# One agenda for every step beside the products, and the first chunk's output through x's buffer: sparse attention followed by a gated network

## The chip, the cores and the metric

The kernel runs on one core of a Trainium2 chip. The metric is the device time of one execution in microseconds. Before the change the median of three runs is 885.96 (885.71 to 888.02).

The core's engines work in parallel, each through its own queue in program order: TensorE (PE) multiplies, VectorE (DVE) and ScalarE (ACT) work element by element, GpSimd (POOL) does too, and SyncE (SP) issues transfers. ACT issues transfers as well, from its own queue. An instruction that waits holds everything behind it on its engine.

## What is computed

```python
# attention: q, k, v of (8 batches, 8 heads, 576, 64), stride 32, scale 1/8
rel = pos[:, None] - pos[None, :]
mask_local   = (rel >= 0) & (rel < 32)                       # heads 0 to 3
mask_strided = (rel >= 0) & (pos[None, :] % 32 == pos[:, None] % 32)   # heads 4 to 7
scores = where(mask, scale * q @ k.T, -1e9)
scores -= max(scores);  attn = exp(scores)
attn /= sum(attn) + 1e-9
x = (attn @ v) laid out as (4608 tokens, 512)

# network: w_in (512, 2048), w_out (2048, 512)
h = x @ w_in
g = where(h >= 1, h, where(h <= -1, 0, (h + 1)**2 / 4))
out = g @ w_out
```

## The kernel before

The network's operands are split into a rounded part and a remainder, and each product is three matmuls (`HI_LO`): high by high, high by low, low by high.

**The network.** The 4608 tokens go in two ways. The first three chunks of 512 tokens (`c` = 0, 1, 2) are done plainly: for each of 16 steps `f`, `up(c, f)` makes one 128-row tile of h in 12 matmuls, `gate` bends it (two activations on ACT, one operation on DVE), `rounded` splits it into `gh` (ACT, in chunks 1 and 2) and `gl` (DVE), and `down` adds it to four output tiles in 12 matmuls. `down` runs two steps behind `up`: `pend` holds the tiles between. h has two PSUM banks, so `up` of a step waits until `gl` of two steps earlier has been read from its bank. `gh` and `gl` have three buffers each, taken by `f % 3`.

The other tokens go in three super-chunks of 1024 (`s` = 0, 1, 2) with a seven-product scheme for 2 by 2 blocks: `up_block` has 56 units of six matmuls, `down_block` 28 units of twelve. Its operands are sums of blocks of x (`x_sum` on DVE, and `x_split`, one cast on ACT and one subtraction on DVE) and sums of blocks of the weights. `prep` makes the operands of `down_block` two units ahead. The weights come back from DRAM through a ring of seven buffers on SP (`fetch_w`).

**Work beside the network in chunks 1 and 2.** The rounded weights of each step are stored to DRAM (`ship`, on ACT's queue). For each of 16 pairs of steps and sides, `combine` makes sums of weight blocks on POOL (two operations of 128x512 and four of 128x256), `round_sums` casts them on ACT, `rest_of_sums` subtracts on DVE, and `ship_sums` stores them from ACT's queue. The room for it is one half of an x buffer (`X0` or `X1`), which held the x of chunk 0 or 1 and later holds that of a super-chunk.

**Attention** for batches 1 to 7 is laid beside the network. A batch has four units: 0 and 1 local, 2 and 3 strided. A step is a letter and a unit: s scores (PE), m mask (DVE, out of PSUM), x maximum (DVE), a or b subtract it (POOL or DVE), e exponential (ACT), q sum (DVE), p or k add eps (ACT or DVE), r or w normalise (a reciprocal on DVE, then POOL or DVE), t transpose (DVE), j store the transposed tile to DRAM and J read it back as pT (both SP), v times the values (PE; V does units 1 and 3), h and l copy the result to x as high and low part (ACT, DVE; l does nothing for tokens of the super-chunks). Scores and values share two PSUM banks, "a": each s, v or V takes both, and the next waits until m, or h and l, have read them.

**What sets the order.** The order on every engine is the order in which the program issues instructions. Time is counted in a unit of six matmuls: step `f` of chunk `c` begins at 4 * (16 * (c - 1) + f), chunk 1 at 0, chunk 2 at 64, the first super-chunk at 128, the second at 240. `LATER` is one table of places for all batches 2 to 7, and `START` says where each batch begins; batches 2, 3 and 4 use b and w in place of a and r. `COMBINE`, `X_FIRST` and `X_NEXT` place the sums and x steps. Within a step of chunks 1 and 2 the order is: `up`; scores and values of the step's first half; `gate`; the first half's other attention steps; `ship`; sums; x steps; `rounded`; the whole `down`; then the second half's steps, sums and x steps. Transfers of q, k and v are issued right behind the step that frees their buffer (`after`).

The output of chunk 0 is copied into three small buffers of the pool `o_p` (which the transposed tiles use too), that of chunk 1 into half 0 of `X1`, that of chunk 2 into a buffer of its own; `put` stores each of the four tiles from SP.

Of the kernel before, what the change touches and what calls it, by code (L numbers as in the profile page):

```python
# [25 lines left out]
def tile_sparse_attention_then_ffn(
# [274 lines left out]

    def fetch_v(b, *parts):
        for u, k in parts:
            if 0 < b < B and (b, UNITS[u][0], UNITS[u][1] + k * VB) not in loaded:
                load_v(b, u, k)


    def attention(b, kinds):
# [256 lines left out]
        def low(u):  # L565
            if u not in flipped:
                return
            for src, to in parts(u):
# [4 lines left out]
        steps = {"s": score, "y": score_0, "z": score_1, "m": mask, "o": opened, "i": cover, "g": plain, "x": most, "w": norm_v, "a": below_max, "e": expo, "q": total, "p": plus_eps, "k": plus_eps_v, "b": below_max_v, "r": norm,
                 "f": flip, "t": turn, "j": spread, "J": gather, "c": keep, "d": keep_v, "v": value, "V": values_1_3, "h": high, "l": low}
        after = {"s1": lambda: fetch_qk(b, 2), "s3": lambda: b > 1 and fetch_qk(b + 1, 0),
                 "v0": lambda: fetch_v(b, (1, 0), (2, 0))}
        if b == 1:
            after |= {"v1": lambda: fetch_v(b, (3, 0)), "v2": lambda: fetch_v(b + 1, (0, 0)), "v3": lambda: fetch_v(b + 1, (0, 1))}
        else:
            after |= {"v2": lambda: fetch_v(b, (3, 0)), "V1": lambda: fetch_v(b + 1, (0, 0), (0, 1))}  # L580
# [59 lines left out]
    def put(rows, cols, t):  # L640
        nc.sync.dma_start(out[rows * P:(rows + 1) * P, cols:cols + CH], t)

    def down(c, f, gs):
        if f == 0:
            o_ps[c] = [psum("o", [P, CH], f"o_{c}_{d}") for d in range(NC)]
        if f == NF - 1 and c:
            room = x_tile(1)[:, 0] if c == 1 else slot(HL_AT[0], [P, NC, CH], F32, f"ob_{c}")
        for d in range(NC):
            h, e = divmod(d * P, HF)
            for n, (x, y) in enumerate(HI_LO):  # L650
                nc.tensor.matmul(o_ps[c][d], wt[f][:, 1, h, x, e:e + P], gs[y],  # L651
                                 start=f == 0 and n == 0, stop=f == NF - 1 and n == 2)
# [231 lines left out]
    with tc.manual_schedule():  # L884
# [38 lines left out]
        goes = {b: attention(b, lambda u, kind, n: "a") for b in range(1, B)}  # L923

        def steps(g0, g1, which):
            for b, g in START.items():
                for at, names in LATER.items():
                    if g0 <= g + at < g1:
                        goes[b](names[which] if b > 4 else names[which].replace("a", "b").replace("r", "w"))

        def x_steps(s, *todo):
            for m in todo:
                x_split(m, s) if m > 0 else x_sum(-m, s)

        COMBINE = {h: (n // NP, n % NP, half) for n, (h, half) in enumerate((
            (0, 1), (2, 0), (5, 1), (7, 0), (10, 1), (12, 0), (15, 1), (20, 1),
            (32, 1), (35, 0), (37, 1), (40, 0), (42, 1), (47, 1), (52, 1), (57, 1)))}

        def sums(h):
            for at, do in ((h - 5, ship_sums), (h - 4, rest_of_sums), (h - 3, round_sums), (h, combine)):
                if at in COMBINE:
                    i, j, half_ = COMBINE[at]
                    do(i, j, x_tile(at // 32)[:, half_])

        X_FIRST = {50: (1,), 52: (2,), 61: (-7, -6, 7), 62: (-4, -5, 6), 63: (5,)}
        pend = []
        for c in range(CLASSIC):
            for f in range(NF):  # L950
# [3 lines left out]
                pe, pre, mid, post = ("",) * 4 if c else STEPS.get(f, ("",) * 4)
                go = goes[1]
                go(pe)
                if c:
                    steps(g0, g0 + 2, 0)
                else:
# [16 lines left out]
                go(post)
                if c:
                    steps(g0, g0 + 2, 1)
                    ship(f, c - 1)
                    sums(g0 // 2)  # L980
                    x_steps(0, *X_FIRST.get(g0 // 2, ()))
                if c:
                    pend.append((c, f, rounded(c, f)))
                if len(pend) > 2:
                    down(*pend.pop(0))
                if c or f == NF - 1:
                    steps(g0 + 2, g0 + 4, 0)
                    steps(g0 + 2, g0 + 4, 1)
                    sums(g0 // 2 + 1)
                    x_steps(0, *X_FIRST.get(g0 // 2 + 1, ()))  # L990
        for n in range(3):
            fetch_w(n)
        for n, a in enumerate(pend):
            down(*a)
# [4 lines left out]
        for s in range(NSC):
            g0 = 4 * NF * (CLASSIC - 1) + 2 * len(UP) * s  # L1000

            def beside(n):
                for which in range(2):
                    steps(g0 + n, g0 + n + 1, which)

            up_block(s, beside)

            def beside_down(n):
                for which in range(2):
                    steps(g0 + len(UP) + 2 * n, g0 + len(UP) + 2 * n + 2, which)  # L1010
                if s + 1 < NSC:
                    x_steps(s + 1, *X_NEXT.get(n, ()))

            down_block(s, beside_down)
# [58 lines left out]
```

## Time and profile before

| what | us |
|---|---|
| median of three runs | 885.96 |
| the profiled execution | 881.21 |
| its span, first to last instruction | 879.1 |
| chunk 1's first step up begins at | 118.89 |
| chunks 1 and 2 take, to the first super-chunk | 251.4 |
| first super-chunk takes | 180.9 |
| second | 169.2 |
| third, to the end of the span | 158.7 |

The stages are read from the begin of each stage's first matmul. The mean granted TensorE clock of the execution is 0.984 of full. The profile's busy time of an engine doesn't tell how fast it worked: a matmul under a low clock is busy longer. A wait is shown with the one that ended it last ("releaser"). A name with an arrow, out<-in, gives the tile written and those read: `h` is a step up, `o` a step down, `sc` scores, `xp` values, `xs` an x buffer in its later use, `hl` the operands of a super-chunk's way down.

### The profile page before, as it was taken

What the parts mean: (1) busy time and instruction counts of PE and PEld (TensorE: products, weight loads), DVE (VectorE), ACT (ScalarE), POOL (GpSimd) and SP (SyncE); (2) the same over time, 40 slices, a digit from 0 to 9 for tenths busy, and PEclk for the clock granted to TensorE, in tenths of its full rate; (3) what the DMA queues carried; (4) which work ended last, traced back from release to release, by engine and by line L of the source; (5) the groups of instructions that cost most, each with busy time, mean ns of one, the idle gap of its engine ahead of it and who ended that gap; (6) DMA issues with size and microseconds to landing.
All of it is one profiled execution on the core that took longest, in us unless ns stands there. A gap on an engine that the chain in (4) does not pass through costs nothing.

```text
span 879.1 us, 17888 instructions
## 1 busy us (share of the span) xinstructions
PE 825.4 (94%) x6965; PEld 662.0 (75%) x6965; DVE 575.3 (65%) x846; ACT 498.6 (57%) x876; POOL 216.0 (25%) x220
## 2 busy tenths in 40 slices
PE   8999998858998899999999989999999899999997
PEld 6688886746876777777877857788888578888885
DVE  6899857655546555855767677566577854467564
ACT  6889835342435534666866533567854437676442
POOL 6364451762025524312321000131110001111000
PEclk9999999978999899999999999999999999999999
DMA  9917226765647865897997846788656567666664
GB/s 354 408 64 271 86 97 236 264 242 190 199 156 257 276 217 213 294 281 242 295 297 232 254 145 225 251 249 241 209 187 215 157 226 210 191 194 190 216 207 141
DMA packets 101795, 195.10 MB, mean 222 GB/s; under 512 B 17104, under 2 KB 32464, under 8 KB 99664
## 3 DMA queue, kind: packets, MB, share of 16 engines
q1 hardware_dynamic: 92496, 164.60, 58.1%
q10 hardware_dynamic: 9216, 29.36, 8.8%
q8 instruction: 55, 0.90, 0.4%
q14 instruction: 28, 0.23, 0.1%
HBM read 147.26 MB, written 46.66 MB: 221 GB/s over the span
## 4 chain that ended last, share of the span: by engine, by line
PE 61%; DVE 18%; ACT 10%; DMA 5%; issue 3%; POOL 1%; SPq 1%; ACTq 0%; DVEq 0%; POOLq 0%
PE y L748 13%; PE h L606 10%; PE o L651 10%; PE yo L849 8%; PE z L748 7%; DVE hl L702 5%; PE xo L849 4%; ACT hl L701 3%; PE x L748 3%; PE xp L507 3%; PE sc L344 2%; DMA pT<-there 2%; DMA ks<-xs 2%; DVE xs L254 1%; DVE xs L698 1%
## 5 line engine op out<-in xcount | busy, mean ns | idle before, releaser
L606 PE MATMUL h<-xq,w 128*128 128x512 f32 x576 | 146.5, 404 | 9.6 <-DVE gl L637 8.8
L748 PE MATMUL y<-x,wr 128*128 128x512 f32 x576 | 140.7, 391 | 0.4 <-ACT ga L756 0.4
L849 PE MATMUL yo<-hl,wr 128*128 128x512 f32 x576 | 135.0, 392 | 3.6 <-DVE hl L702 3.6
L606 PEld LDWEIGHTS h<-xq,w 128*128 128x128 f32 x576 | 109.9, 194 | 36.8 <-DVE gl L637 11.0
L651 PE MATMUL o<-gh,w 128*128 128x512 f32 x384 | 131.9, 405 | 0.5 <-ACT ob L655 0.5
L849 PEld LDWEIGHTS yo<-hl,wr 128*128 128x128 f32 x576 | 107.3, 188 | 29.2 <-DVE hl L702 6.5
L748 PEld LDWEIGHTS y<-x,wr 128*128 128x128 f32 x576 | 107.6, 188 | 23.6 <-ACT ga L756 0.9
L651 PEld LDWEIGHTS o<-gh,w 128*128 128x128 f32 x384 | 74.0, 193 | 18.0 <-ACT ob L655 1.4
L849 PE MATMUL zo<-hl,wr 128*128 128x512 f32 x288 | 69.8, 395 | 8.5 <-DVE hl L702 4.6
L651 PE MATMUL o<-gl,w 128*128 128x512 f32 x192 | 76.4, 398 | 0.4 <-DVE gl L637 0.4
L748 PE MATMUL z<-x,wr 128*128 128x512 f32 x288 | 74.3, 393 | 1.7 <-ACT gab L783 1.3
L245 POOL TENSOR_TENSOR xs<-w 128x512 f32<-128x512 f32 x32 | 44.8, 1421 | 113.5 <-DMA ks<-xs 66.1
L849 PEld LDWEIGHTS zo<-hl,wr 128*128 128x128 f32 x288 | 53.3, 188 | 24.4 <-DVE hl L702 7.5
L702 DVE TENSOR_TENSOR hl<-ga,hl 128x1024 fp32r<-128x1024 f32 x36 | 45.0, 1249 | 40.2 <-ACT hl L701 40.2
L616 DVE SCALAR_TENSOR_TENSOR h<-h,u 128x512 f32<-128x512 f32 x47 | 32.8, 697 | 54.8 <-ACT u L613 54.5
L701 ACT CAST hl<-ga 128x1024 fp32r<-128x1024 f32 x36 | 38.0, 1055 | 53.2 <-DVE ga L802 29.4
L748 PEld LDWEIGHTS z<-x,wr 128*128 128x128 f32 x288 | 53.4, 188 | 13.8 <-ACT gab L783 1.8
L613 ACT ACTIVATE tmp<-tmp 128x512 f32<-128x512 f32 x96 | 60.7, 632 | 3.1
L788 POOL TENSOR_TENSOR ga<-gb,ga 128x1024 f32<-128x1024 f32 x9 | 21.6, 2405 | 165.5 <-DVE ga L616 157.7
L410 POOL TENSOR_TENSOR pr<-pr,st 128x768 f32<-128x768 f32 (+3 forms) x19 | 23.6, 1242 | 136.3 <-DVE st L406 135.4
L247 POOL TENSOR_TENSOR xs<-xs 128x256 f32<-128x256 f32 x64 | 54.6, 853 | 5.0
L610 ACT ACTIVATE u<-h,half 128x512 f32<-128x512 f32 x48 | 32.8, 684 | 36.5 <-PE h L606 27.4
(117 smaller groups left out, 1310.3 us busy)
## 6 DMA issues: line engine op xcount, KB each, us to landing
wr<-ks SPq DMA_DIRECT2D x192, 256.0 KB, 3.7
wr<-kq SPq DMA_DIRECT2D x144, 256.0 KB, 3.0
ks<-xs ACTq DMA_DIRECT2D x16, 1024.0 KB, 4.1
raw<-in_w SPq DMA_DIRECT2D x30, 512.0 KB, 9.6
kq<-w ACTq DMA_DIRECT2D x48, 256.0 KB, 3.2
qk<-in_qk_s SPq DMA_DIRECT2D x16, 604.0 KB, 6.3
qk<-in_qk_l SPq DMA_DIRECT2D x16, 576.0 KB, 6.0
v<-in_v_l SPq DMA_DIRECT2D x21, 384.0 KB, 5.1
```

The costliest lines, as they stand in the source:

```text
L245: nc.gpsimd.tensor_tensor(out=b[:, :, f] if i else b[:, f], in0=hi, in1=lo, op=ALU.add)
L247: nc.gpsimd.tensor_tensor(out=st[:, to, HF:], in0=st[:, x, HF:], in1=st[:, y, HF:], op=op)
L507: nc.tensor.matmul(xp[p][j * D:(j + 1) * D, n], loaded[b, local, b0 + n][keys, j], qs, start=True, stop=True)
L606: nc.tensor.matmul(o_ps[c, f], wt[f][:, 0, h, x, e:e + P], xq[c][:, y, cc], start=first and n == 0, stop=last and n == len(todo) - 1)
L610: nc.scalar.activation(u, h, AF.Relu, bias=half, scale=0.5)
L613: nc.scalar.activation(u, u, AF.Square)
L616: nc.vector.scalar_tensor_tensor(out=to, in0=h, scalar=1.0, in1=u, op0=ALU.max, op1=ALU.min)
L651: nc.tensor.matmul(o_ps[c][d], wt[f][:, 1, h, x, e:e + P], gs[y], start=f == 0 and n == 0, stop=f == NF - 1 and n == 2)
L701: nc.scalar.copy(t[:, 0], src)
L702: nc.vector.tensor_tensor(out=t[:, 1], in0=src, in1=t[:, 0].bitcast(F32), op=ALU.subtract)
L748: nc.tensor.matmul(to, w_[:, a, c * P:(c + 1) * P], xc[m][:, b, c], start=m in (1, 2, 5) and c + q == 0, stop=c == 1 and q == 2, skip_grou ...
L849: nc.tensor.matmul(to, w_[jj][:, a, d * P:(d + 1) * P], t[:, b, jj], start=m in (1, 2, 5) and k + jj + q == 0, stop=k == NP // 2 - 1 and j ...
```

## The change

Every step that stands beside the products gets a time of its own in one agenda, in the same unit. `WORK` holds the attention steps of each batch, and the transfers of q and k (Q) and v (F) as steps too; `SUMS` the half of the x buffer and four times for each pair; `X_WORK` the x steps; `SHIP` the stores of the weights. All are sorted into one list, and `until(t)` issues what stands before t. In a step of chunks 1 and 2 this happens at five places: between `up` and `gate`, between `gate` and `down`, in the middle of `down` (now in two halves), between `down` and `rounded`, and behind `rounded`. In the super-chunks it happens behind each unit. Batch 1 and chunk 0 keep their order. `k` (eps on DVE) takes the place of `p` (ACT) in 12 of 24 units. Chunk 0's output goes through half 0 of `X0`.

```diff
+GATE, ROUNDED, BEFORE_BLOCKS = 2.04, 3.18, 128.01
+WORK = {2: [(0, 's0 m0 x0 b0'), (2.67, 'e0'), (5.15, 'q0'), (5.57, 's1'), (6, 'Q2 k0 w0 m1 x1 a1'), (9, 't0 e1'),
+     (9.7, 'q1'), (11, 'j0'), (11.93, 'k1'), (11.98, 'w1'), (12, 's2 m2 x2 b2'), (14, 'J0'), (14.93, 't1'),
+     (15, 'e2'), (16.33, 'v0 h0'), (16.93, 'j1'), (18.28, 'l0'), (18.41, 'F2'), (20, 'F3'), (21.43, 'q2'),
+     (22, 's3 m3 x3 b3 k2 w2'), (23.4, 'J1'), (25, 't2 e3'), (26.56, 'j2'), (29, 'q3 k3 w3'), (30.33, 'J2'),
+     (36.67, 't3'), (36.87, 'v2 h2 l2'), (38.87, 'j3'), (40.27, 'F4'), (41.32, 'J3'), (46.4, 'V1 h1'), (46.72, 'l1'),
+     (46.87, 'h3 l3')],
+ 3: [(22.01, 'Q0'), (36.73, 's0 m0 x0'), (36.83, 'b0'), (39.73, 'e0'), (41.37, 'q0'), (41.38, 's1'),
...
+     (66.05, 'J2'), (68.2, 'w3'), (70.45, 't3'), (72.41, 'v2 F4'), (72.83, 'j3'), (73.4, 'h2 l2'), (77.23, 'J3'),
+     (83.17, 'V1 h1 l1'), (83.29, 'h3'), (87.11, 'l3')],
+ 4: [(58.99, 'Q0'), (73.01, 's0 m0 x0 b0'), (76.79, 'e0'), (78.77, 's1'), (78.91, 'q0 k0'), (79.01, 'm1 x1 b1'),
+     (80.05, 'Q2'), (81.29, 'w0'), (81.54, 't0'), (81.82, 'e1'), (83.47, 'F0'), (83.91, 'j0'), (84.35, 's2'),
...
+     (118.15, 'V1 h1 l1'), (118.37, 'h3'), (120.2, 'l3')],
+ 5: [(97.96, 'Q0'), (114.25, 's0 m0 x0 a0'), (117.76, 'e0'), (117.77, 'q0'), (118.94, 'F0'), (119.93, 'p0'),
+     (120.08, 'F1'), (121.05, 'r0'), (121.07, 's1 Q2 m1 x1 a1'), (123.43, 't0'), (124.93, 'j0'), (126.1, 'e1'),
...
+     (144.07, 'p3'), (144.43, 'J2'), (149.71, 'r3'), (150.15, 'v2 h2 l2'), (150.17, 't3'),
...
+ 6: [(138.46, 'Q0'), (152.07, 's0 m0 x0 a0'), (155.07, 'e0'), (157.89, 'q0 k0 r0'), (158.07, 's1 m1 x1 a1'),
...
+SUMS = [((0, 0), 8.6, 15.07, 16.58, 17.74), ((1, 1), 84.6, 91.54, 92.6, 94.96), ((0, 1), 10.6, 17.05, 18.6, 20.6),
+ ((0, 0), 19.07, 24.98, 26.89, 28.2), ((0, 1), 21.03, 28.67, 29.03, 31.03), ((0, 1), 33.13, 36.6, 36.86, 40.16),
+ ((0, 0), 28.38, 33.33, 33.99, 36.48), ((1, 0), 73.13, 76.42, 76.84, 80.6), ((1, 1), 105.13, 111.18, 111.62, 115.13),
+ ((0, 1), 41.28, 48.8, 49.22, 51.26), ((1, 1), 74.6, 80.6, 80.86, 84.51), ((1, 0), 83.39, 87.41, 88.1, 90.6),
+ ((0, 1), 0.4, 6.18, 7.79, 10.18), ((1, 1), 95.44, 100.22, 102.87, 103.32), ((1, 1), 62.86, 63.55, 67.17, 72.94),
+ ((1, 1), 118.76, 122.36, 124.36, 127.05)]
+X_WORK = {0: [(103.03, 1), (106.03, 2), (122.41, -7), (123.8, -6), (123.8, 7), (126.73, -5), (127.38, 5), (127.44, 6),
+     (128.28, -4), (129.16, 3), (129.21, 4)],
+ 1: [(205.07, 1), (206.28, 2), (207.03, -7), (208.7, -6), (213.43, 7), (214.81, -4), (215.28, -5), (218.35, 6),
+     (218.77, 5), (224.13, 3), (237.21, 4)],
+ 2: [(316.65, -7), (317.01, 1), (318.58, -6), (319.18, 2), (321.64, 7), (325.62, -4), (325.64, -5), (330.83, 6),
+     (333.72, 5), (336.7, 3), (348.73, 4)]}
...
-    def down(c, f, gs):
-        if f == 0:
+    def down(c, f, gs, ds=range(4)):
+        if f == 0 and 0 in ds:
...
-        if f == NF - 1 and c:
-            room = x_tile(1)[:, 0] if c == 1 else slot(HL_AT[0], [P, NC, CH], F32, f"ob_{c}")
-        for d in range(NC):
+        if f == NF - 1 and 0 in ds:
+            outs[c] = x_tile(c)[:, 0] if c < 2 else slot(HL_AT[0], [P, NC, CH], F32, f"ob_{c}")
+        for d in ds:
...
-                ob = room[:, d] if c else o_p.tile([P, CH], F32, tag="ob", name=f"ob_{c}_{d}")
-                nc.scalar.copy(ob, o_ps[c][d])
-                put(d, c * CH, ob)
+                nc.scalar.copy(outs[c][:, d], o_ps[c][d])
+                put(d, c * CH, outs[c][:, d])
...
+        agenda.sort(key=lambda a: a[:2])
+
+        def until(t):
+            while agenda and agenda[0][0] < t:
+                _, _, do, what = agenda.pop(0)
+                do(*what)
...
+                until(t + GATE)
+                gate(c, f)
+                until(t + 2)
+                gs = pend.pop(0)
+                down(*gs, (0, 1))
+                until(t + 3)
+                down(*gs, (2, 3))
+                until(t + ROUNDED)
+                pend.append((c, f, rounded(c, f)))
+                until(t + 4)
...
+        until(BEFORE_BLOCKS)
         for s in range(NSC):
+            t = 4 * NF * (CLASSIC - 1) + 2 * len(UP) * s
+            up_block(s, lambda n: until(t + n + 1))
+            down_block(s, lambda n: until(t + len(UP) + 2 * n + 2))
```

More of the change, by code (lines that the diff above doesn't have):

```diff
@@ L22 @@
 CLASSIC = 3
+GATE, ROUNDED, BEFORE_BLOCKS = 2.04, 3.18, 128.01
+WORK = {2: [(0, 's0 m0 x0 b0'), (2.67, 'e0'), (5.15, 'q0'), (5.57, 's1'), (6, 'Q2 k0 w0 m1 x1 a1'), (9, 't0 e1'),
[40 rows of a table added]
+SUMS = [((0, 0), 8.6, 15.07, 16.58, 17.74), ((1, 1), 84.6, 91.54, 92.6, 94.96), ((0, 1), 10.6, 17.05, 18.6, 20.6),
[5 rows of a table added]
+X_WORK = {0: [(103.03, 1), (106.03, 2), (122.41, -7), (123.8, -6), (123.8, 7), (126.73, -5), (127.38, 5), (127.44, 6),
[4 more added lines that the diff above has]
+     (333.72, 5), (336.7, 3), (348.73, 4)]}
+SHIP = [[2.64, 5.47, 9.9, 19.19, 11.97, 21.72, 26.64, 29.9, 33.9, 34.97, 40.51, 47.24, 49.62, 48.01, 57.9, 63.22],
+ [65.9, 74.24, 64.69, 76.21, 81.97, 85.9, 87.99, 93.9, 97.9, 103.72, 106.71, 110.82, 113.67, 117.9, 121.64, 125.9]]
 @with_exitstack
@@ L573, in attention @@
         steps = {"s": score, "y": score_0, "z": score_1, "m": mask, "o": opened, "i": cover, "g": plain, "x": most, "w": norm_v, "a": below_max, "e": expo, "q": total, "p": plus_eps, "k": plus_eps_v, "b": below_max_v, "r": norm,
[L574 to L580, printed above, removed]
+                 "f": flip, "t": turn, "j": spread, "J": gather, "c": keep, "d": keep_v, "v": value, "V": values_1_3, "h": high, "l": low,
+                 "Q": lambda p: fetch_qk(b, p), "F": lambda n: fetch_v(b, ((0, 0), (0, 1), (1, 0), (2, 0), (3, 0))[n])}
+        after = {"s1": lambda: fetch_qk(b, 2), "v0": lambda: fetch_v(b, (1, 0), (2, 0)), "v1": lambda: fetch_v(b, (3, 0)),
+                 "v2": lambda: fetch_v(b + 1, (0, 0)), "v3": lambda: fetch_v(b + 1, (0, 1))}
         def go(names):
@@ L587, in go @@
                 steps[name[0]](int(name[1]))
-                if b:
+                if b == 1:
                     after.get(name, int)()
         return go
-    o_ps = {}
+    o_ps, outs = {}, {}
     def up(c, f, first=True, last=True):
@@ L914, in tile_sparse_attention_then_ffn, with x_step, sum_step @@
                  14: ("v3", "", "", "h3 l3")}
-        START = {2: 0, 3: 37, 4: 73, 5: 115, 6: 152, 7: 240}
-        LATER = {0: ("s0", "m0 x0 a0"), 3: ("", "e0"), 6: ("s1", "q0 p0 r0 m1 x1 a1"), 9: ("", "t0 e1"), 11: ("", "j0"),
[4 rows of a table removed]
-        goes = {b: attention(b, lambda u, kind, n: "a") for b in range(1, B)}
[L925 to L947, printed above, removed]
+        goes = {b: attention(b, lambda u, kind, n: "a") for b in range(1, B)}
+        def x_step(s, m):
+            x_split(m, s) if m > 0 else x_sum(-m, s)
+        def sum_step(n, step):
+            s, half_ = SUMS[n][0]
+            i, j = divmod(n, NP)
+            (combine, round_sums, rest_of_sums, ship_sums)[step](i, j, x_tile(s)[:, half_])
+        agenda = [(t, 0, goes[b], (name,)) for b, work in WORK.items() for t, names in work for name in names.split()]
+        agenda += [(t, 1, sum_step, (n, step)) for n, (_, *ts) in enumerate(SUMS) for step, t in enumerate(ts)]
+        agenda += [(t, 2, x_step, (s, m)) for s, work in X_WORK.items() for t, m in work]
+        agenda += [(t, 3, ship, (f, i)) for i, ts in enumerate(SHIP) for f, t in enumerate(ts)]
+        agenda.sort(key=lambda a: a[:2])
[3 more added lines that the diff above has]
+                do(*what)
         pend = []
@@ L950, in tile_sparse_attention_then_ffn @@
             for f in range(NF):
-                g0 = 4 * (NF * (c - 1) + f)
+                t = 4 * (NF * (c - 1) + f)
                 if c or f > 1:
                     up(c, f)
[L954 to L959, printed above, removed]
+                if c == 0:
+                    pe, pre, mid, post = STEPS.get(f, ("",) * 4)
+                    go = goes[1]
+                    go(pe)
                     start_w(*halves[f])
-                go(pre)
-                gate(c, f, lambda: go(mid))
-                if c == 0:
+                    go(pre)
+                    gate(c, f, lambda: go(mid))
                     pend.append((c, f, rounded(c, f)))
-                if c == 0:
                     end_w(*halves[f])
@@ L975, in tile_sparse_attention_then_ffn @@
                         fetch_qk(2, 0)
[L976 to L990, printed above, removed]
+                    go(post)
+                    if len(pend) > 2:
+                        down(*pend.pop(0))
+                    until(t + 4)
+                    continue
+                until(t + GATE)
[7 more added lines that the diff above has]
+                pend.append((c, f, rounded(c, f)))
+                until(t + 4)
         for n in range(3):
@@ L996, in tile_sparse_attention_then_ffn @@
                 fetch_w(3 + 2 * n + at)
-        x_steps(0, 3, 4)
-        X_NEXT = {10: (1,), 11: (2,), 12: (-7, -6), 13: (7,), 14: (-4,), 15: (-5,), 16: (6,), 18: (5,), 20: (3,), 27: (4,)}
+        until(BEFORE_BLOCKS)
         for s in range(NSC):
[L1000 to L1014, printed above, removed]
+            t = 4 * NF * (CLASSIC - 1) + 2 * len(UP) * s
+            up_block(s, lambda n: until(t + n + 1))
+            down_block(s, lambda n: until(t + len(UP) + 2 * n + 2))
 _OUTS = [((512, 4608), "float32")]
```

30 rows, old and new, of tables (LATER, WORK) are left out of this document.

## The prediction

> **What bounds the kernel now.** Three views, in this order: the summary, the busy time by stage, the waits of the matmul queue. Times are microseconds from the span's start. In the second fence the columns are the stretch, its length, then busy time of PE, PEld, DVE, ACT and POOL, the granted clock, DMA share and GB/s. The stretches are: chunks 1 and 2 ("classic" from here on), then the three super-chunks.
>
> ```profile
> span 879.1 us, 17888 instructions
> PE 825.4 (94%) x6965; PEld 662.0 (75%) x6965; DVE 575.3 (65%) x846; ACT 498.6 (57%) x876; POOL 216.0 (25%) x220
> PEclk9999999978999899999999999999999999999999
> ```
> ```profile
> 118.90:370.30 251.40, 223.76 (x2376) 177.89 (x2376) 149.57 (x236) 107.25 (x208) 102.42 (x106) 0.95 0.63 220
> 370.30:551.20 180.90, 171.18 (x1409) 136.08 (x1408) 123.26 (x163) 107.73 (x182) 25.37 (x19) 1.00 0.79 248
> 551.20:720.40 169.20, 163.96 (x1137) 131.91 (x1137) 114.33 (x145) 99.91 (x157) 19.89 (x14) 1.00 0.70 216
> 720.40:879.10 158.70, 153.44 (x673) 125.74 (x671) 89.06 (x102) 88.00 (x125) 9.62 (x4) 1.00 0.62 194
> ```
> ```profile
> 118.89 2.72 PE h L606 x12
> L344 PE MATMUL sc<-qk 64*32 64x64 f32 (+1 forms) x1856 | 33.3, 231 | 15.2 <-DVE xq L570 6.9 <-ACT xs L561 4.7 <-DMA qk<-in_qk_s 2.9
> L507 PE MATMUL xp<-pT,v 64*64 64x32 f32 (+2 forms) x1760 | 32.9, 221 | 7.7 <-DMA pT<-there 4.4 <-DVE pr L395 1.7 <-issue 0.8
> ```
> ```profile
> 875.21 0.59 ACT L825 COPY last<-yo 128x512 f32<-128x512 f32 x1 [0.74 <-PE yo L849]
> ```
>
> TensorE bounds it, but a PE that is "94% busy" isn't full. Twelve matmuls of the network take 2.72 at full rate, so one takes 0.227. Classic holds 32 steps up and 34 steps down of 12 each, 792 matmuls, 179.5. Attention: scores 33.3 and values about 33 over eight batches, so 8.3 a batch; classic holds three batches and three score units of a fourth, about 29. That is 208.5 of work in 251.4, so 43 are lost. A super-chunk has 672 matmuls, 152.3. The last one, with no attention beside it, ends its matmuls when the last copy starts, 154.8 after its start: 2.5 lost, and a tail of 3.9. The second has one batch (160.6 of work in 169.2, 8.6 lost), the first about 1.6 batches (165.9 in 180.9, 15.0 lost). The places that a reordering can mend are therefore mostly in classic, and the waits there are:
>
> ```profile
> PE h L606 <- DVE gl L637: 8.8, 5, 2.5
> PE sc L344 <- DVE xq L570: 6.9, 1, 6.9
> PE sc L344 <- ACT xs L561: 3.6, 3, 2.3
> PE xp L507 <- DMA pT<-there: 3.3, 3, 1.7
> PE sc L344 <- DMA qk<-in_qk_s: 2.0, 2, 1.1
> PE xp L507 <- DVE pr L395: 1.7, 1, 1.7
> ```
>
> Together 26.3 idle. The rest of the 43 is a low clock behind those gaps (0.95 granted over 251.4 is 12.6) and small restarts. The rows that carry it, idle time and releaser in brackets:
>
> ```profile
> 132.51 3.02 PE L606 MATMUL h<-xq,w 128*128 128x512 f32 x12 [0.70 <-DVE gl L637]
> 177.91 4.59 PE L606 MATMUL h<-xq,w 128*128 128x512 f32 x12 [2.49 <-DVE gl L637]
> 195.94 2.16 PE L344 MATMUL sc<-qk 64*32 64x64 f32 x96 [6.93 <-DVE xq L570]
> 219.38 4.59 PE L606 MATMUL h<-xq,w 128*128 128x512 f32 x12
> 259.19 3.02 PE L606 MATMUL h<-xq,w 128*128 128x512 f32 x12 [1.40 <-DVE gl L637]
> 262.15 1.17 PE L344 MATMUL sc<-qk 64*32 64x64 f32 x96
> 327.63 4.61 PE L606 MATMUL h<-xq,w 128*128 128x512 f32 x12 [2.00 <-DVE gl L637]
> 288.93 2.02 PE L344 MATMUL sc<-qk 64*64 64x54 f32 x48 [2.31 <-ACT xs L561]
> ```
> ```profile
> 198.10 4.93 PE o L651 x12
> 290.95 4.62 PE o L651 x12
> ```
>
> Twelve matmuls that take 4.6 to 4.9 instead of 2.72 stand behind the gaps: the gap is paid a second time.
>
> **The change, part by part.** One unit of the agenda is six matmuls, 1.36; its zero is 118.89. No matmul, cast or transfer is added or taken away. The only arithmetic that changes engine: twelve of the 24 additions of eps go from ACT to DVE (k for p), four subtractions of the maximum (a for b) go from DVE to POOL in batches 2 to 4, one the other way in batch 6, and two normalisations (w for r) from POOL to DVE. Each is a microsecond or less on engines that are 43 to 60% busy in classic: nothing by itself. What matters is order.
>
> (1) Batch 2's v2 and batch 3's s0 had one place (37). Both need the two banks "a", so s0 waited until h2 and l2 had read v2's result: 6.93 idle, then 2.16 for 1.17 and 4.93 for 2.72, 10.1 in all. Now s0 (36.73) stands ahead of v2 (36.87), with m0 between. v2 then waits for m0; the nearest row is the 1.7 of xp behind pr, which is this same order at batch 4. h2 stands behind a store of x's buffer, but nothing on PE asks for the banks before s1 at 41.38. **Saved 8.4.** Bounds: nothing left of it (10.1), or as much again as xs cost at 288.93 (2.3, saving 7.8).
>
> (2) Five waits for gl, of which 0.70 and 1.40 stand at the chunk joints. The other three come to 6.7, and two of them are followed by 4.6 instead of 2.72, so 3.8 more. What held gl:
>
> ```profile
> ACT st L425 <- DVE st L421: 29.5, 12, 5.7
> ACT xs L250 <- POOL xs L247: 22.3, 7, 5.1
> ACT gh L634 <- PE o L651: 14.9, 2, 8.1
> POOL xs L245 <- DMA out<-xs: 15.9, 1, 15.9
> L247 POOL TENSOR_TENSOR xs<-xs 128x256 f32<-128x256 f32 x64 | 54.6, 853 | 5.0
> L245 POOL TENSOR_TENSOR xs<-w 128x512 f32<-128x512 f32 x30 | 42.2, 1429 | 109.5 <-DMA ks<-xs 66.1 <-DVE pr L395 17.8 <-DMA out<-xs 15.9
> L254 DVE TENSOR_TENSOR xs<-xs 128x1024 fp32r<-128x1024 f32 x16 | 22.8, 1424 | 0.0
> ```
>
> ACT stood 29.5 for sums on DVE before it could add eps, and 22.3 for POOL's sums of weights before rounding them, with the casts of gh queued behind. With k the first goes in batches 2 to 4 for all but two units. The second: a combine is 2 x 1.43 + 4 x 0.85 = 6.3, or 4.6 units, and most rounds now stand 5 to 7.6 units behind their combine; those of sums 5, 7, 11, 14 and 15 stand closer and still make ACT wait, but a gate has about 8 units until the next but one step up. One new wait: chunk 0's output takes half of x's buffer 0, and the combine at 8.6 must wait until its four stores have landed. ACT's copies run behind gh(1,0), which waits until down(0,15) ends at about 8, so the last store lands near 14. That combine then ends near 18.6 and the next (10.6) near 23, whose round (17.05) is queued ahead of gate(1,4); gl(1,4) comes about a unit late for the step up at 24. I leave 2.0 for that. **Saved 10.5 - 2.0 = 8.5**; bounds 10.5 and 4.
>
> (3) Q2 moves ahead of the stores of chunk 0's output on SP, and these no longer wait for three small buffers, so batch 2's strided q and k come before s2. **Saved 2.0**; bounds 2.0 and 0.
>
> (4) pT. J3 to V1 stays at about 5 units, so most of the 3.3 stays, and v0 of batch 2 comes only 2.3 units behind J0. I leave 3.0; the 1.9 of slow matmuls behind it (219.38) go, as no two gaps then stand together. **Saved 2.2**; bounds 5.2, and a loss of 2.
>
> (5) sc behind xs, 3.6. V1 of batch 4 (118.15) now has three units before the next scores (121.07): 1.3 saved. V1 and s2 at 83.17 and 84.35 stay as close as they were, so 2.3 and the slow matmuls behind stay. **Saved 1.3**; bounds 3.6 and 0.
>
> (6) The joints. gh(1,0) takes the buffer of gh(0,15), because 16 steps are not a multiple of three, and ACT waits 8.1 for it. The change leaves this alone. s1 no longer fills the hole (5.57, ahead of it), so 1.4 instead of 0.7 at unit 8; at 72 the same, and s0 behind v2 waits for h2 instead of v2 behind m0, 2.0 instead of 1.7. **Lost 0.5 to 1; I take 0.5.**
>
> (7) Super-chunks:
>
> ```profile
> 411.81 0.30 PE L344 MATMUL sc<-qk 64*32 64x64 f32 x2 [0.80 <-ACT xs L561]
> PE zo L849 <- DVE hl L702: 2.3, 3, 0.8
> PE zo L849 <- ACT hl L701: 1.9, 3, 0.6
> L698 DVE TENSOR_TENSOR xs<-xs 128x1024 f32<-128x1024 f32 x4 | 4.8, 1208 | 0.0
> ```
>
> s0 of batch 6 had v2's place and now has two units: about 1.1 saved. In product 5 of the way down DVE is the slow engine, and each x step of 1.2 that falls among its four units is paid; the second super-chunk now has two of these in place of four: 2.4 of its 4.2. In the first there are three, and two more close behind: nothing. **Saved 3.5.**
>
> The stores of the rounded weights (ship) and v's loads (F) go to other places on ACT's queue and SP's. Each is one issue; what hides them is that nothing reads them for tens of units. If F stands ahead of its free buffer it holds SP, and in the super-chunks the weights behind it, which are seven units ahead, 9.5.
>
> **Sum:** 8.4 + 8.5 + 2.0 + 2.2 + 1.3 - 0.5 + 3.5 = 25.4. The profiled execution took 881.21 (span 879.1); the median of the runs is 885.96. Taken from the median: **860.6**; the profiled execution would be about 856.
>
> [...] In (1), (2) and (4), 8.9 of the saving are slow matmuls behind gaps. After 2.49 idle, twelve took 4.59, yet after 0.70 and 1.40 they took 3.02. [...]
>
> **Rivals.**
> A. The gaps that I left (joints 3.4 and 1.4, m0 1.7, gl 2.0, pT 3.0, xs 2.3 with 3.0 of slow clock, product 5's 1.8) vanish too, 18.6: 842. For it: DVE and ACT are far from full. Against: the joint's buffer is untouched.
> B. The slow stretches don't hang on the short gaps: 25.4 - 5.7 saved, 866. For it: a gap of 0.70 or 1.40 left twelve matmuls at 3.02, so idle time alone need not slow them. Against it: each slow stretch stands right behind a longer gap.
> C. Only the plain collisions go, (1) and (3), 10.4, and gl's waits come back elsewhere: 875.6. For it: each place was moved alone, and in-order queues hand a wait on.
> D. Slower: x's buffer. If chunk 0's stores land after unit 14, POOL's seven combines from 8.6 to 41.28 run back to back (one every 5.4 units on average, against their own 4.6), each round holds ACT ahead of a gate, and each costs what the row at 177.91 shows, 2.49 + 1.87 = 4.4. Seven are 30.5: 860.6 + 30.5 = 891. It decides where POOL's first combine on half 0 starts later than about 14; the wait of 15.9 for out<-xs at chunk 1 speaks for it, the pause before the combine at 19.07 against it.
> E. The order of each queue hardly differs, since steps are still let in at only five places of a step, and nothing moves: 886. Against it: (1) and (3) change places on PE's and SP's own queues.
>
> **Chances.** Forecast 0.50, A 0.18, B 0.10, C 0.10, D 0.07, E 0.05. A difference under 0.3%, 2.7, can't be told from none. Faster 0.88, same 0.05, slower 0.07. The range 840 to 880 holds the forecast with the bounds of its terms and A to C.
>
> **What would show it.** Right: between 188 and 203 no gap over 2 and no stretch under clock 0.8; ACT's wait for L421 in classic well under 10; classic about 229 long; gl's waits only at the joints and near unit 25; the zo waits still in the first super-chunk. Wrong: POOL's first combine on half 0 late and gates behind its rounds; gaps of over 2 at new places; wr the releaser of PE in the super-chunks.

## The result, and the profile after

The changed kernel takes 859.44 (median of four runs, 857.27 to 860.75); the kernel before, timed beside it, 885.84. The ratio is 0.9706, with a 95% interval of 0.9663 to 0.9749: 26.0 faster, against 25.4 forecast (860.6, range 840 to 880). A second timing of the same kernel gave 0.9707 (0.9682 to 0.9731).

The profiled execution took 859.13, 22.1 less than that of the kernel before (881.21), which was one of that kernel's faster ones. Its summary, then the busy time by stage (columns as before: stretch, length, PE, PEld, DVE, ACT, POOL, granted clock, DMA share, GB/s), for the changed kernel:

```profile
span 857.3 us, 17861 instructions
PE 821.8 (96%) x6965; PEld 660.9 (77%) x6965; DVE 575.5 (67%) x857; ACT 496.1 (58%) x864; POOL 215.5 (25%) x221
PEclk9999999999999999999999999999999999999999
```
```profile
120.85:350.65 229.80, 215.85 (x2377) 172.58 (x2376) 146.55 (x242) 105.23 (x198) 106.44 (x109) 0.99 0.69 241
350.65:532.27 181.62, 173.47 (x1505) 138.27 (x1504) 125.48 (x167) 107.38 (x181) 22.60 (x17) 0.99 0.80 248
532.27:698.71 166.44, 162.62 (x1046) 131.09 (x1041) 115.05 (x146) 99.69 (x156) 18.20 (x13) 1.00 0.72 219
698.71:857.30 158.59, 153.45 (x673) 125.75 (x671) 89.06 (x102) 87.98 (x125) 9.60 (x4) 1.00 0.64 194
```

Busy time of the vector engines hardly moved; the stage of chunks 1 and 2 went from 251.4 to 229.8. Part of that lies in the clock column: by its rounded figures, 0.95 over 251.4 is 12.6 lost to a low clock and 0.99 over 229.8 is 2.3. Added up from the slow stretches themselves it is 12.3 and 4.0, so about two fifths. The first super-chunk is 0.7 longer, the second 2.8 shorter, the third 0.1.

Chunk 0 took 2.0 longer in this profile (chunk 1 begins at 120.85, not 118.89), though its order didn't change. The same matmuls in the same order took longer there (eleven transposes on PE, at 19.54 and at 21.11, took 1.42 and then 2.61), and the stretch 20 to 27, for the kernel before and then for the changed one, shows that it is the clock (eighth number):

```profile
20.00:27.00 7.00, 5.76 (x108) 4.02 (x106) 5.75 (x21) 5.43 (x22) 2.19 (x2) 1.00 1.02 411
```
```profile
20.00:27.00 7.00, 7.00 (x149) 6.25 (x145) 4.96 (x17) 3.99 (x17) 3.11 (x3) 0.71 1.02 413
```

Over all profiles of this study chunk 1 begins anywhere between 118.1 and 121.4, in kernels old and new. So a difference of 3 in one profile's span says nothing, and the experiments below are read by stage and by wait, and timed by ratio.

The waits of PE in chunks 1 and 2 of the changed kernel, and four of ACT's:

```profile
PE h L665 <- DVE gl L696: 5.3, 4, 2.3
PE xp L569 <- DVE pr L457: 4.0, 1, 4.0
PE sc L406 <- ACT xs L623: 2.9, 4, 1.7
PE xp L569 <- DMA pT<-there: 0.8, 1, 0.8
PE o L710 <- DVE gl L696: 0.6, 1, 0.6
```
```profile
ACT gh L693 <- DVE h L675: 30.1, 22, 4.4
ACT xs L312 <- POOL xs L309: 26.9, 9, 4.9
ACT gh L693 <- PE o L710: 10.9, 2, 5.5
ACT st L487 <- DVE st L483: 3.4, 2, 3.2
```

The first four rows are 13.0 idle, in place of 26.3; the last, 0.6, was 0.4 before. ACT's wait to add eps fell from 29.5 to 3.4, as forecast. Its wait for POOL's sums rose from 22.3 to 26.9, and that for the gate's product on DVE from 12.0 to 30.1; neither was forecast. The rows with a gap, in order of time, with batch 3's s0 (185.37) between:

```profile
135.45 3.01 PE L665 MATMUL h<-xq,w 128*128 128x512 f32 x12 [1.40 <-DVE gl L696]
152.08 1.59 PE L569 MATMUL xp<-pT,v 64*64 64x32 f32 x92 [0.83 <-DMA pT<-there]
182.43 3.01 PE L665 MATMUL h<-xq,w 128*128 128x512 f32 x12 [2.34 <-DVE gl L696]
185.37 1.17 PE L406 MATMUL sc<-qk 64*32 64x64 f32 x96
190.50 1.79 PE L569 MATMUL xp<-pT,v 54*64 54x64 f32 x48 [3.96 <-DVE pr L457]
252.49 0.30 PE L406 MATMUL sc<-qk 64*32 64x64 f32 x2 [0.79 <-ACT xs L623]
275.10 0.32 PE L406 MATMUL sc<-qk 64*64 64x54 f32 x2 [1.73 <-ACT xs L623]
362.83 0.30 PE L569 MATMUL xp<-pT,v 64*64 64x32 f32 x4 [2.13 <-DMA pT<-there]
499.07 0.50 PE L907 MATMUL zo<-hl,wr 128*128 128x512 f32 x1 [1.67 <-ACT hl L759]
```

The first joint costs the 1.4 that was forecast (135.45), v0 of batch 2 0.8. The place that I called the largest gain is still the largest gap: v2 behind m0, 3.96. Two slow stretches are left in chunks 1 and 2: the step down behind that gap (4.1 in place of 2.72), and the one behind the wait of 1.73 at 275.10, which ran from 276.43 to 280.87 with 0.62 of the clock:

```profile
276.43:280.87 4.44, 4.44 (x17) 3.53 (x13) 3.72 (x7) 2.22 (x4) 3.75 (x4) 0.62 1.09 323
```

### The profile page after: what moved, and what is told of

It reads as the page before. It is cut to its first block, busy times and chain, and to the rows that moved or that the text cites. A ratio compares the mean times of both kernels' runs of the same rounds, so it can differ in the third digit from the quotient of the medians.

```text
span 857.3 us, 17861 instructions
## 1 busy us (share of the span) xinstructions
PE 821.8 (96%) x6965; PEld 660.9 (77%) x6965; DVE 575.5 (67%) x857; ACT 496.1 (58%) x864; POOL 215.5 (25%) x221
## 4 chain that ended last, share of the span: by engine, by line
PE 68%; DVE 16%; ACT 8%; DMA 3%; POOL 2%; issue 2%; ACTq 0%; POOLq 0%; DVEq 0%
PE y L806 14%; PE o L710 12%; PE h L665 11%; PE yo L907 8%; PE z L806 7%; DVE hl L760 5%; PE xo L907 4%; ACT hl L759 4%; PE xp L569 3%; PE x L806 3%; PE sc L406 2%; DVE xs L756 1%; DVE ga L860 1%; DVE gb L862 1%; POOL xs L309 1%
## 5 line engine op out<-in xcount | busy, mean ns | idle before, releaser
L665 PE MATMUL h<-xq,w 128*128 128x512 f32 x576 | 140.9, 393 | 6.1 <-DVE gl L696 5.3
L806 PE MATMUL y<-x,wr 128*128 128x512 f32 x576 | 143.1, 393 | 0.1
L665 PEld LDWEIGHTS h<-xq,w 128*128 128x128 f32 x576 | 107.5, 188 | 32.0 <-DVE gl L696 7.3
L472 POOL TENSOR_TENSOR pr<-pr,st 128x384 f32<-128x384 f32 (+3 forms) x22 | 25.5, 1159 | 182.6 <-DVE st L468 182.3
L846 POOL TENSOR_TENSOR ga<-gb,ga 128x1024 f32<-128x1024 f32 x9 | 21.6, 2397 | 174.3 <-DVE ga L675 159.2
L309 POOL TENSOR_TENSOR xs<-xs 128x256 f32<-128x256 f32 x64 | 52.2, 815 | 5.0
```

Source lines behind the costliest of these rows:

```text
L309: nc.gpsimd.tensor_tensor(out=st[:, to, HF:], in0=st[:, x, HF:], in1=st[:, y, HF:], op=op)
L665: nc.tensor.matmul(o_ps[c, f], wt[f][:, 0, h, x, e:e + P], xq[c][:, y, cc], start=first and n == 0, stop=last and n == len(todo) - 1)
L806: nc.tensor.matmul(to, w_[:, a, c * P:(c + 1) * P], xc[m][:, b, c], start=m in (1, 2, 5) and c + q == 0, stop=c == 1 and q == 2, skip_grou ...
```

## Experiments

A time is the median; the ratio is to the kernel before, timed in the same session.

**Where do the 2.34 and the 3.96 come from?** ACT's, then DVE's and POOL's rows around them in the changed kernel:

```profile
177.03 1.05 ACT L312 CAST xs<-xs 128x1024 fp32r<-128x1024 f32 x1 [4.86 <-POOL xs L309]
184.82 1.05 ACT L312 CAST xs<-xs 128x1024 fp32r<-128x1024 f32 x1 [3.17 <-POOL xs L309]
```
```profile
185.90 1.23 DVE L316 TENSOR_TENSOR xs<-xs 128x1024 fp32r<-128x1024 f32 x1 [3.53 <-ACT xs L312]
187.15 0.70 DVE L675 SCALAR_TENSOR_TENSOR h<-h,u 128x512 f32<-128x512 f32 x1
188.50 0.69 DVE L696 TENSOR_TENSOR gl<-h,gh 128x512 fp32r<-128x512 f32 x1 [0.65 <-ACT gh L693]
189.11 0.89 DVE L533 STREAM_TRANSPOSE t<-pr 128x320 f32<-128x320 f32 x2
189.93 0.98 DVE L457 TENSOR_TENSOR pr<-sc,m_loc 128x384 f32<-128x384 f32 x2
```
```profile
178.05 3.50 POOL L307 TENSOR_TENSOR xs<-w 128x512 f32<-128x512 f32 x2 [0.93 <-DMA ks<-xs]
```

s0's scores are ready at 186.5 (185.37 and 1.17), but m0 (189.93) is the fifth row from the remainder of a sum of weights (185.90) on, which waits for ACT's round (184.82), which waits for POOL's sum. The gate's activations stand behind that round on ACT, so the gate's product (187.15) is late with it. The 2.34 goes the same way with the sum and the round before (177.03). POOL itself began the later sum (178.05) when the store of an earlier one out of the same room had landed. Three theories of why the sums are late: J, the buffer of gh at the chunk joint; X, the stores of chunk 0 out of x's buffer; S, the chain POOL, ACT, DVE, store of the sums itself.

**joint**

```diff
-        gh, gl = (short(n + f % 3, F32R, f"{a}_{c}_{f}") ...
+        gh, gl = (short(n + (c + f) % 3, F32R, f"{a}_{c}_{f}") ...
-    RING_AT = (1, 4, 6, 2, 5, 0, 3)
+    RING_AT = (0, 3, 6, 1, 4, 2, 5)
```

> The changed kernel, with gh's and gl's buffers taken by a running count over the chunks, so that gh(1,0) no longer needs the buffer of gh(0,15), and the ring of weights reordered to suit. In the changed kernel four waits for gl stand in chunks 1 and 2 (1.40 and 0.15 at the first joint, 2.34, 1.40 at the second), one of 3.96 of v2 behind m0, and ACT waits 10.9 for the step down before gh. Theory J (the joint's buffer starts the chain that ends in 2.34 and 3.96): all of these go or fall under 1 each, chunks 1 and 2 take about 219 to 222 in place of 229.8, about 850 in all. Theory X (the stores of chunk 0 out of x's buffer start it): only the 1.40 and 1.40 go, 227, about 857. Theory S (the sums' own chain of POOL, ACT, DVE and store is too long for its places, whatever comes before): 1.40, 0.15 and 1.40 go, 2.34 and 3.96 stay, 227.

853.20, ratio 0.9658 (0.9627 to 0.9690), some 4 faster than the changed kernel, with intervals that overlap a little. Chunks 1 and 2 took 226.1. PE's waits there:

```profile
PE xp L569 <- DVE pr L457: 5.2, 1, 5.2
PE h L665 <- DVE gl L696: 1.4, 2, 1.3
PE sc L406 <- ACT xs L623: 1.0, 2, 0.8
```

The 1.40 at both joints are gone, and so is the 1.73 behind V1 of batch 3; the 2.34 fell to 1.3, but v2 now waits 5.2. The two at unit 36 together stay (6.3 before, 6.5 now): J explains its own 2.8, and as the start of the 2.34 and 3.96 it is not borne out. (This profile also has a gap of 1.67 at 252.93 that has no releaser.) POOL's first sum on half 0 of `X0` was done only 1.4 earlier, though, counted from chunk 1's begin. The subtraction ahead of it was 5.6 earlier, but now the sum waited for the stores of chunk 0's output, 3.64 and 1.26:

```profile
133.33 0.83 POOL L472 TENSOR_TENSOR pr<-pr,st 128x384 f32<-128x384 f32 x1 [9.63 <-DVE st L468]
137.80 1.29 POOL L307 TENSOR_TENSOR xs<-w 128x512 f32<-128x512 f32 x1 [3.64 <-DMA out<-xs]
```

So joint takes away the first hindrance and meets the second, that of theory X.

**outbuf**

```diff
-        if f == NF - 1 and 0 in ds:
+        if f == NF - 1 and 0 in ds and c:
...
-                nc.scalar.copy(outs[c][:, d], o_ps[c][d])
-                put(d, c * CH, outs[c][:, d])
+                ob = outs[c][:, d] if c else o_p.tile([P, CH], F32, tag="ob", name=f"ob_{c}_{d}")
+                nc.scalar.copy(ob, o_ps[c][d])
+                put(d, c * CH, ob)
```

> The changed kernel with chunk 0's output back in the three small buffers: the agenda without x's buffer. Theory X: POOL's first combine no longer waits for stores, the waits of 2.34 and 3.96 shrink by more than half, 4 to 6 faster than the changed kernel, about 854. Theories J and S: POOL's first combine is held by a subtraction of batch 2 queued ahead of it, not by the stores, so these waits stay within 0.5; the fourth copy waits for the first store, which may cost up to 1 on PE as before the change (0.46). About 859 to 861.

859.90, ratio 0.9731 (0.9705 to 0.9756): no gain, and the same gaps (2.10 and 3.96). X alone falls. The output through x's buffer, the second half of the change's title, neither earns nor costs anything that these runs can tell. POOL's first sum on that half began at 140.07 in the changed kernel, right behind a subtraction for batch 2 that had waited 15.25 for DVE. It is one of the four that the change moves from DVE to POOL. In the changed kernel POOL waited for stores of output twice in this stage, neither time before 160, so not for chunk 0's:

```profile
139.28 0.83 POOL L472 TENSOR_TENSOR pr<-pr,st 128x384 f32<-128x384 f32 x1 [15.25 <-DVE st L468]
140.07 3.53 POOL L307 TENSOR_TENSOR xs<-w 128x512 f32<-128x512 f32 x2
```
```profile
POOL xs L307 <- DMA out<-xs: 17.5, 2, 16.6
```

No run takes away J and X together, and in none of these did POOL's first sum come much earlier. S is what is left when each is removed alone; that the sums would be late with both removed is not shown.

**roundlate**

```diff
- ... ((0, 1), 21.03, 28.67, 29.03, 31.03), ((0, 1), 33.13, 36.6, 36.86, 40.16),
- ((0, 0), 28.38, 33.33, 33.99, 36.48), ...
+ ... ((0, 1), 21.03, 31.2, 31.5, 33.03), ((0, 1), 33.13, 39.2, 39.5, 40.16),
+ ((0, 0), 28.38, 35.2, 35.5, 36.48), ...
```

> The changed kernel with three sums' rounds and remainders moved behind the casts of gh of their step (28.67 to 31.2, 33.33 to 35.2, 36.6 to 39.2, the remainders 0.3 later, two stores likewise), so that ACT no longer stands before POOL's sum with a gate behind it. Theory S: the 2.47 before the step up and the 3.96 of v2 behind m0 fall under 1.5 each, with the low clock behind: 4 to 7 faster than the changed kernel. Rival: the sums are then late for x's buffer and h2 and V1 wait for their stores: within 1.5.

858.50, ratio 0.9718 (0.9684 to 0.9752), the same as the changed kernel. One of the two gaps went and the other took its length:

```profile
PE xp L569 <- DVE pr L457: 6.7, 1, 6.7
PE h L665 <- DVE gl L696: 2.8, 2, 1.4
```

With the rounds out of the gates' way gl is on time (2.8 are the two joints), and m0 is later by what gl gained. What holds m0 is no longer a late POOL sum. The two rounds started without a wait for POOL, and ACT's waits for POOL's sums in chunks 1 and 2 fell from 26.9 to 17.4. Now the store of a sum stands on ACT's queue ahead of a gate, and it goes out only when DVE's remainder ends, at 179.29; the gate's activations, whose h was ready at 175, follow at 181.16:

```profile
179.33 0.33 ACTq L319 DMA_DIRECT2D ks<-xs  x1
181.16 0.69 ACT L669 ACTIVATE u<-h,half 128x512 f32<-128x512 f32 x1 [4.21 <-issue]
```

So the edit itself, which moved the stores too, put a later link of the sums' chain in the gate's way. It bears out S as far as S names the store, and not that POOL's part is what is late.

**v2late**

```diff
-     (36.67, 't3'), (36.87, 'v2 h2 l2'), (38.87, 'j3'), ...
+     (36.67, 't3'), (38.87, 'j3'), (39.1, 'v2'), (39.2, 'h2 l2'), ...
```

> The changed kernel with v2 of batch 2 moved from 36.87 to 39.1, behind that step's whole way down, and h2 and l2 to 39.2. Theory S (m0 is held on DVE behind the remainder of a sum whose POOL part is late, so v2 stands in front of work that PE could do): PE does the 12 matmuls down in that time, the gap of 3.96 and the slow matmuls behind it (2.2) go, 4 to 6 faster than the changed kernel. Rival: the lateness is only handed on, to gl and the next step up, and 3 or more appear there: within 1.5 of it.

855.10, ratio 0.9685 (0.9661 to 0.9708), 1 to 2 faster than the changed kernel, which the interval can't tell from none. The gap of 3.96 fell to 0.97, and a new one of 1.66 came at s1 of batch 3, which now stands behind l2: handed on by nearly half, with a step down of 4.6 behind it.

```profile
188.66 1.38 PE L569 MATMUL xp<-pT,v 54*64 54x64 f32 x48 [0.97 <-DVE pr L457]
194.66 0.30 PE L406 MATMUL sc<-qk 64*32 64x64 f32 x2 [1.66 <-DVE xq L632]
```

**collide**

```diff
-  ... (36.73, 's0 m0 x0'), (36.83, 'b0'), ...
+  ... (36.88, 's0 m0 x0'), (36.89, 'b0'), ...
```

> The changed kernel with s0, m0, x0 and b0 of batch 3 put back behind v2, h2 and l2 of batch 2 (36.88 in place of 36.73). If my term (1) is right in kind, s0 waits for h2 and l2 again: a gap of 6 to 7 with a low clock behind, in place of 3.96 with 2.2 behind, so 3 to 5 slower than the changed kernel, about 863. If the collision wasn't what the place cost (the rival: both orders wait for the same late sums on ACT and DVE), the gap is 4 to 5 and the time the same within 1.5.

858.80, ratio 0.9737 (0.9695 to 0.9778), against 0.9706: not settled. In its profiled execution, itself one of 865.12 where the other three took 857.7 to 859.0, the gap was 9.12:

```profile
195.05 2.04 PE L406 MATMUL sc<-qk 64*32 64x64 f32 x96 [9.12 <-DVE xq L632]
```

So the order of s0 and v2 decides the gap in this one execution, but the timed runs don't show the 3 to 5 that it should cost: by the ratios it is 2.7 slower, with intervals that overlap. Late sums are in this gap as well. The copies h2, for which s0 waits, stood behind a round that had waited 2.85 for POOL.

**before_apart**

```diff
-        START = {2: 0, 3: 37, 4: 73, 5: 115, 6: 152, 7: 240}
+        START = {2: 0, 3: 39, 4: 73, 5: 115, 6: 152, 7: 240}
```

> The kernel before with one number changed: batch 3 begins at 39 in place of 37, so that its s0 stands a half step behind v2 of batch 2 (37), with h2 and l2 between. It undoes the collision of term (1) alone. If that term is right, the 6.93 and the slow matmuls behind it go but for some 2: 6 to 9 faster than before, 874 to 877. If the sums on POOL, ACT and DVE are what was late there, as v2late showed for the changed kernel, s0 or the next step up waits as well: 0 to 3 faster.

883.01, ratio 0.9992 (0.9971 to 1.0014): nothing. Twelve matmuls between v2 and s0 did not undo the collision. h2 had to wait until the store of a sum had landed, 1.87 in the kernel before and 3.46 here. And shifting the batch made other waits longer (gl 11.3 for 8.8):

```profile
PE h L606 <- DVE gl L637: 11.3, 5, 3.8
PE sc L344 <- DVE xq L570: 5.6, 1, 5.6
```
```profile
197.24 0.34 ACT L561 COPY xs<-xp 128x108 f32<-128x108 f32 x1 [3.46 <-DMA ks<-xs]
```

**before_k**: the old kernel's batches 2 to 4 with `k` for `p`.

```diff
-  ... names[which].replace("a", "b").replace("r", "w"))
+  ... names[which].replace("a", "b").replace("r", "w").replace("p", "k"))
```

> The kernel before with eps added on DVE (k for p) in batches 2 to 4 and nothing else. My term (2) laid the waits of gl to ACT's 29.5 of standing before it can add eps: if that holds, that wait goes and the gaps of 2.21, 2.49 and 2.00 before a step up shrink by half or more, 3 to 7 faster. Rival: ACT then stands at the next thing, the rounding of the sums (22.3 before, 26.9 after the change), and the gaps stay: 0 to 2 faster.

878.24, ratio 0.9948 (0.9927 to 0.9970): 4.6 faster by itself. gl's waits before a step up fell from 8.8 to 5.2; of the three away from the joints 2.21 and 2.00 are gone and 1.59 and 1.48 remain, and a wait of 1.94 for gl came ahead of a step down. That part of term (2) is shown.

**before_joint**: the edit of joint in the kernel before.

> The kernel before, with the running count for gh's and gl's buffers and the ring reordered, nothing else. Theory J: ACT's 14.9 of waiting for the step down goes, with the waits for gl of 0.70 and 1.40, and the two of 2.2 and 2.5 behind the first joint shrink: 4 to 8 faster than before, 878 to 882. Theory S: only the 2.1 at the joints goes, 883 to 885.

875.91, ratio 0.9912 (0.9885 to 0.9939): 7.8 faster; whether that is more than in the changed kernel (4.3) the intervals can't tell. Chunks 1 and 2 took 244.7 in place of 251.4. The time is what theory J said, its mechanism is not: the waits for gl before a step up came to 8.4 in place of 8.8 (2.69, 1.41, 1.47 and 2.81). Gone are the 0.70 and the 1.40, the 1.72 of xp behind m0 at the second joint, and the 2.0 for q and k.

**xmove**

```diff
- 1: [(205.07, 1), (206.28, 2), (207.03, -7), (208.7, -6), (213.43, 7), (214.81, -4), (215.28, -5), (218.35, 6),
-     (218.77, 5), (224.13, 3), (237.21, 4)],
+ 1: [(200.1, -7), (202.1, 1), (204.1, 2), (206.1, -6), (208.1, 7), (210.1, -4), (210.2, -5), (220.1, 6),
+     (222.1, 5), (224.13, 3), (237.21, 4)],
...
```

> The changed kernel with the x steps of the second and third super-chunk moved so that none falls on units 14 to 17 of the way down before them: the sums and the first splits one a unit from unit 8 on, the later splits from unit 18. My term (7) says that each x step of 1.2 among product 5's preparations is paid: the waits of zo, 3.15 and 2.4, fall under 1 each, about 4 faster than the changed kernel. Rival: product 5 alone is too slow on DVE (a subtraction, a cast, a subtraction of 3.5 against 2.72 of matmuls), and half or more of the waits stay: 0 to 2 faster.

854.19, ratio 0.9679 (0.9653 to 0.9705), 2.5 under the changed kernel's, with intervals that overlap. The waits of zo and of the product's end fell from 3.15 to 1.75 in the first super-chunk and from 2.3 to 1.8 in the second; what stays is one short wait a unit, as here:

```profile
490.93 3.06 PE L907 MATMUL zo<-hl,wr 128*128 128x512 f32 x12 [0.50 <-DVE hl L760]
```

More than half of the waits stay, as the rival said: x steps among product 5 are paid in part, and product 5 alone is a little too slow too.

**after_again** (the changed kernel as a mark), **best** (joint, v2late, xmove, J0 of batch 5 at 128.5, s0 of batch 4 behind h2 of batch 3) and **best2** (best with roundlate).

```diff
-      ... (130.07, 't1'), (130.18, 'J0'),
+      ... (130.07, 't1'), (128.5, 'J0'),
-      ... (72.41, 'v2 F4'), (72.83, 'j3'), (73.4, 'h2 l2'), ...
+      ... (72.41, 'v2 F4 h2 l2'), (72.83, 'j3'), ...
-  4: [(58.99, 'Q0'), (73.01, 's0 m0 x0 b0'), ...
+  4: [(58.99, 'Q0'), (75.1, 's0'), (75.2, 'm0 x0 b0'), ...
```

> The changed kernel itself, as the mark for the runs beside it: 858 to 861, with the 3.96 of v2 behind m0 and about 3 of waits in each of the first two super-chunks' product 5.

> All together: the running count for gh's buffers, v2 late, the x steps moved, J0 of batch 5 at 128.5 in place of 130.18 (its wait of 2.6 at v0), and s0 of batch 4 at 75.1, behind h2 of batch 3. If each wait is its own, 6 + 5 + 4 + 2 + 1 = 18 faster than the changed kernel, about 841. If the waits are handed on, 846 to 851.

> The joined version of before with the rounds moved as well. Theory S: its 1.48 and 2.10 go, 3 to 4 faster than 843: 839 to 840. Rival: handed on, 842 to 844.

856.46 (ratio 0.9707), 843.27 (0.9553, 0.9531 to 0.9575) and 841.14 (0.9514, 0.9483 to 0.9546). best gains 13.6 on the changed kernel by the ratios (0.0154 of 884); joint (4.3), v2late (1.9) and xmove (2.5) alone come to 8.7. Its two other moves have no run of their own; going by the waits that went with them, 1.6 at v0 of batch 5 and 1.0 at s0 of batch 4, they are worth some 2.6. Both best and best2 came out between what the two forecasts for each had said. In best2 chunks 1 and 2 took 218.5, and the longest of PE's waits there are:

```profile
PE xp L569 <- DVE pr L457: 3.2, 2, 2.0
```

roundlate, worth nothing alone, has a ratio 0.004 lower on top of best, with intervals that overlap a little. That moves which hand a wait on alone pay once the next in line has been moved too fits this and the 13.6 against 8.7 and 2.6, but the difference is within the intervals: it is likely, not shown.

## Why the prediction was right, and which steps were mis-sized

The total and the stage are right: 21.9 was forecast for chunks 1 and 2, 21.6 came; 3.5 for the super-chunks, 2.1 came. So the way is right: reordering made the waits in chunks 1 and 2 and the slow stretches behind them fewer. Inside, sizes were off and made up for each other, which is luck: (1) fell 4.5 short, and (4), (5) and (6) brought 4.7 more than forecast.

| term | forecast | in the profiles |
|---|---|---|
| (1) v2 and s0 | 8.4 | 3.9: of 10.1 are left 3.96, and 0.9 and 1.4 of slow matmuls behind it |
| (2) gl | 8.5 | 8.0: of 10.5 are left 2.34 and 0.15 |
| (3) q and k | 2.0 | 2.0 |
| (4) pT | 2.2 | 4.3: of 5.2 is left 0.83 |
| (5) sc behind xs | 1.3 | 3.0: of 6.6 with its slow matmuls are left 1.73, 0.18 and 1.7 of slow matmuls |
| (6) joints | -0.5 | 0.4: 0.70, 1.40, 1.72 and 0.45 of slow matmuls became 1.40, 1.40 and 1.04 |
| (7) super-chunks | 3.5 | 2.1 |

(1) is the step that was mis-sized: 3.9 lies under both of its bounds (7.8 and 10.1). Its kind holds in the profiles (with s0 first the gap is 3.96, with v2 first 9.12 in the one profile of it), but what I set for the wait behind m0, 1.7 from the same order at batch 4, left out what stands ahead of m0 on DVE: the remainder of a sum, 3.5 late. The row 22.3 of ACT behind POOL was in my own fence; I read it for gl alone. So the first of the prediction's signs failed: a gap of 3.96 ends at 190.50, and the stretch from there to 196.40 has a clock of 0.71. And before_apart shows that moving the collision apart by half a step, without the rest, would have earned nothing.

(2) was right in size and half right in cause. k alone brings 4.6 in the kernel before. The 2.34 that stayed is not chunk 0's stores, as I put it, and not near unit 25: it is a late sum, ahead of the step up at unit 36. That the 2.0 set aside for one is close to the size of the other is luck, and so is that no slow stretch followed the 2.34: at the same place of xmove, whose chunks 1 and 2 are the same, it did.

(4) and (5) were forecast too small: pT came in time at V1 although J3 stands no earlier, and the scores behind V1 of batch 3 wait 1.9 in place of 2.3 and are no longer slow themselves (1.1 saved), with the slow step down behind them still there, as forecast; the other scores behind xs, 1.3 before, no longer wait. (7): the second super-chunk brought 2.8 against 2.4; in the first, s0's place brought its 1.1, but v0 of batch 5 lost 1.6 to a pT that J0's later place (130.18) made late, 2.13 and 0.45 at 362.83 against 1.0 before, a gap of over 2 at a new place, with six matmuls of 2.74 in place of 1.52 behind it. In best, with J0 at 128.5, it is 0.46 and 0.49.

Of the rivals, A did not come: the joints' gaps stayed, as its "against" said, and joint shows that they could go. C did not come either, though the single experiments look like its reason: waits are handed on. D came in small: the first sum was held not by the stores but by a subtraction, one of the four whose move to POOL was put at nothing (they took 0.83 to 1.28 there); what that costs no run shows. Rounds did hold ACT ahead of gates, and that is the 2.34 and the 3.96. In joint, the stores held the first sum too. B's total of 866, which leaves out the 3.8 of slow matmuls in (2) and the 1.9 in (4), is above what was measured (857.27 to 860.75): gaps over 2 became fewer, and of five slow stretches in chunks 1 and 2 two are left.

## What to carry to other kernels

Follow a wait on the matmul queue back through each in-order queue to the first instruction that was late; here late POOL sums showed as a wait for gl, for m0 or for h2, by who stood behind them. An edit that only reorders such a queue should be expected to move the wait (2.34 and 3.96 became 6.71 in roundlate), and the row that holds the queue has to be found anew after each edit, since it can be another one. A buffer taken by an index that restarts in each chunk (16 steps, three buffers) made a wait of 1.40 at both joints, which this agenda left and a running count took away.

## What the runs showed of the hardware that wasn't expected

Gaps of nearly one length were followed by slow matmuls in one execution and not in another. After 2.34 in the changed kernel twelve took 3.01, and after 2.10 at the same place of outbuf 3.02; after 2.11 at that place of xmove they took 4.39, under a granted clock of 0.65, and after 2.69 in before_joint 4.32. The rows of xmove and outbuf:

```profile
180.00 4.39 PE L665 MATMUL h<-xq,w 128*128 128x512 f32 x12 [2.11 <-DVE gl L696]
```
```profile
180.65 3.02 PE L665 MATMUL h<-xq,w 128*128 128x512 f32 x12 [2.10 <-DVE gl L696]
```

Behind V1 of batch 3, where only 48 small matmuls of scores stand between the gap and the step down, it is the same: after 1.39 in both, the granted clock in the 4.6 that begin with the step down was 0.63 in outbuf and 1.00 in roundlate.
